# A second order of issue for a two-layer attention and token-mixing kernel: every operation's place and engine replaced by another list

## The chip, the core and the metric

The kernel runs on one core of a Trainium2 chip. A core has five engines with a queue of instructions each: TensorE (PE in the profile; its weight loads are shown as PEld), VectorE (DVE), ScalarE (ACT), GpSimd (POOL) and SyncE (SP), which here issues all DMA transfers. Engines wait for one another through semaphores. Matmul results go to PSUM, which has eight banks of 128 x 512 f32; everything else is in SBUF or in HBM.

The metric is the time of one execution on the device in microseconds; the median of several runs is compared. A profile is one further execution.

## The reference

Two kinds of block, each applied twice, with a residual: A is attention with a sliding window of 256 positions in 32 heads of 16 channels, B mixes over the 2048 positions (tokens), not over the channels.

```python
def _A_ref(x, wqkv, wo):
    B, S, D = x.shape                      # 1, 2048, 512
    H = 32; Dh = D // H; W = 256
    qkv = (x @ wqkv).reshape(B, S, 3, H, Dh).transpose(2, 0, 3, 1, 4)
    q, k, v = qkv[0], qkv[1], qkv[2]
    scores = jnp.einsum("bhqd,bhkd->bhqk", q, k) * (Dh ** -0.5)
    idx = jnp.arange(S)
    mask = (idx[:, None] - idx[None, :] >= 0) & (idx[:, None] - idx[None, :] < W)
    p = softmax(where(mask, scores, -1e9))
    o = jnp.einsum("bhqk,bhkd->bhqd", p, v)
    return o.transpose(0, 2, 1, 3).reshape(B, S, D) @ wo

def _B_ref(x, w1, b1, w2, b2):             # w1: 2048 x 1792, w2: 1792 x 2048
    h = layernorm(x)
    u = gelu(jnp.einsum("bsd,sf->bdf", h, w1) + b1)
    y = jnp.einsum("bdf,fs->bds", u, w2) + b2
    return y.transpose(0, 2, 1)

x = A_x
x = x + A(layernorm(x)); x = x + B(layernorm(x))
x = x + A(layernorm(x)); x = x + B(layernorm(x))
```

All inputs and the output are bfloat16.

## The kernel before

The activations x stay in SBUF (`x_sb`, 16 tiles of 128 positions). Each of the two layers is one A and one B.

*Attention.* The sixteen tiles are taken in four groups of 512. `qkv` (L530) transposes the normalised tiles (by DMA, or for the first group by PE with an eviction, L544, L551, L553), multiplies them with wqkv (`mm_group`, whose matmuls all stand under L508) and evicts q, k and v from PSUM. K is expanded to a block-diagonal form `kbd`, so that two heads share 32 rows: by POOL or DVE (`f_kz2`, L603) or by eight small DMA transfers on SP (`f_kz`, L598). V goes to `vb` by DMA (L628). `attention` (L656) then works in score groups: 8, 12 or 24 small matmuls into four banks (L682), two exponentials on ACT (L697), masks on POOL (L718), and, once several groups are there, the product with V (L735). The product's result is transposed, normalised and transposed again (L755 to L766, on DVE, with the multiplication on POOL or DVE). `wo_block` adds the output projection to x (L777) and begins the next normalisation.

*Token mixing.* `u_part` (L830) multiplies the normalised tiles that are there with pieces of w1, which SP loads into four buffers (`load_w1`, L791), and collects partial sums (L841, L843, L845). `u_last` (L849) does the rest, L856, and the gelu (L871). `y_block` (L889) multiplies with w2 (`load_w2`, L803) and adds to x (L897). y of layer 0 is made between the attention work of layer 1. So PE always has dense matmuls (all under L508 and L856) that can be put between the score groups.

*What sets the order.* The program first describes 2471 operations, each with its reads, writes and one to three ways of doing it (engine and function). Then a list that is written out in the file decides everything: `ORDER`, a compressed text, gives for each place in the order which of the operations left comes next and which of its ways is taken.

```python
for lo, hi in zip(raw[:n], raw[n:]):
    k, alt = divmod(lo + 256 * hi, 4)
    out.append((left.pop(k), alt))
```

`Graph.replay` (L175) goes through this list once. It appends each operation to the queue of its engine and gives it buffers and PSUM banks, as a rule those that have been free longest; whoever used a buffer last is added to what the operation waits for. `emit` (L196) writes the queues out with the semaphore waits that are needed (L242). So one list sets the order on five engines, the engine of each operation that has a choice, the order of the DMA transfers on SP's queue, and which bank each matmul group takes over from whom. The functions `mm_cost` to `pool_cost` (L253 to L265) play no part when the list is replayed.

Of the kernel before, what the change touches and what calls it, by code (L numbers as in the profile page):

```python
# [7 lines left out]
dt = mybir.dt  # L8
# [3 lines left out]
P = 128  # L12


ORDER = (
    'c-pmAJ&5br6~40X?7Q#nO}GI)P@x3{?t&H+(1HS5&;t=vsL+BI^uUD+2VA&tp@0`uxKQE31QjkE@Pdm8DB!|{3l}aNaN)v*3l}b?aN)v*3l}B~!Nmk}W'
    'Y2i)_hy&u%kCMCbfx=yzVn^$SnedODN2knQDjVp+hTzTLQLETf#aB><9Od%mi3M?<Bv@LI(W~R#HwZM-OBrR37wYfj;FKfJL}zKI<ekLOg9W^&=<wGB3'
    'R=#6~%)nwmRL-rY(OlolcVRY&xHdZ<Ch!jrmPC41BQ~iekCUzpNF4g3m0|v?rw^Hu#saOt_|LTvIvUP)eo!WHN!LEXxSPpQ@^amdmVOVhwR$y+16!*wJ'
    '}uJ`XnAcxyYhedpBcb)=ii^?EHy(u6P2LQxL<FyK2r9HeQ#M|Znj4FF*LcZyP3EEn?yg-M}4&bAs1M&r>~QP^NeBq?~`Znr6IJ8`eqlbO`$-gen$6Pnc'
    '|5%qY^8qHE>f38O5N_nxUR;$xc3aj-}R9?U)rA=|Sds7Vuwc1GKy;@kU(sEj<_`c_r$}q9+!6}16P|`F>EqIFW*wRLl?;!-{d~T-oH^gy9qmgK5ws!2l'  # L20
    'F*b(dDVnZDk*4XoLSa)?(*gi4g9nDuVzH;2w`4pXTXwf=iK1@6rMFrwLI6VuyGXk<j$@J}2qj4ZXwYh9u-R-_zdxnqw|Kp}%WSjV-fcI5?fbhutQ^Oyc'
    'zu7r_V)jBoVEA*-i_yz@hFb*axpOHi$UKs$78eG?GA<m*EM$zi_;!suIu)aq}go3UiG?EF2`}BRyUHwI2>BWzR@6XFs)vX%b8WHl_kcd5-yiVBUCCu_}'
    'w7z;i1W@YOFVFa8*-*xnPn61k{y*qI@Mu;{)9(NlV7fX1ha36i1HZ)M|b$3@a^Y`Z26li!v-dS!QqnyPcz{B104dGF)BFxDLh@rG-*LahggPuoJVqsn>'
    'G~R{(Ne84W8C2u_GhB+(Wn(-b9HlDMS!@I7lv<Tb+>bCn+s=x``xR93u5RxI1L3Iyn`X^<N`NJSVfGcoO_SsHaZ9kh86(EZw{gb1h}^(Xy4LVY#jLsLM'
    'VPNm)Mv}xu)WG_Z`Ba|dcb>>S5DJbjEXl5mv>I$b)wU-Tzuo5&-093_Oby6(3Zd*ery-jFrnz3m+u8SGwT=i5}byQ79Xyv$jWJ{`U@UbK@8TVvmIJE0b'
    'Y}LdCQ$#0<Sgn@IAy}bMu;LN~IErXZR1m=IsweZl&62lIdcARPG*UR6ir?P0l;1;CzkmykoC?^eQrS_|YPYmnO^g0e`#x^Okny$zYyjP;h7%YMevtvBP'
    'mz$pU{I|(z^a5yJis)H5~c52#YPwwi<L^D0K<ZyAZ6%K0%5Ui_=k)T33*KjB!!OAe!FjiDrovfTjP~s8mrX;lxs`@S<oEROK)#GwEdu%5aLFo0cs>!mL'
    'v@+>1&<N59kM#X!>8ZY(I?s@^{~9dW`W+?R!N5W!di5+v$|y#bPwsZnw5Qv?2fQR<QbfHlIu*ux<q5fqX?Sr2!p|+@WPNHk-{fL<P%&gDW6~-4>+?Qsp'
    '(``+GnJ7H=!cLYe0p4VJVL)@SwJc-(BVM%e3BR5eK62Wspa<tQy?0jkG!4<pw{UX}s~o2KV@t|N*L^C*BKdAjMCmY&Jy+A^(~X&7HQt^*Q!a6Namx{H_'
    'THvNb6cRu2rgGw2ex#D+sHC;C?$cn12iPS72I2kCErU4_g_ZoP;4Z~r!r~=vm$;0{lPxIMK*C(8}Rkbi24M!2E#Ar0cu<GDzV>U|*0gU5QKtYmao7e<*'  # L30
    'JMH%Uy}fVkK#%*t=>QJh?znDJPhfT&!>cNa6)`9W1tX|bE8c3g^SmXH#4$ipTnkb!C?tv6<PSbBaM!h6jQ<S}&x1nbh>)+EWm}lIvl()yQ&-yU2(i}4g'
    'hGWf4Fc7LsH<&Fqlk0g4}6@-kTtPnG=%c^aKJb87DLEZtJboGF_gjC4A#YHI2n&akj6n84u`{8x0^svT;xF23TqHRjEk75QKYIv-z%3rRw`p`V_%YLzU'
    '70EnPxq+EHzy<3<(kqN>#@G^B^k^4-bq|Xc)%Cw)gj0gjYyZJEa-$49eVm{LgWgi-TiE-a;)S{XXaEmrc}YpjMpt6+-H9^p~g}Mc646#)SevSSm7zNul'
    '8TmUYLllIfk6m1u4wdDao%3RS2g1`;BUkbof3#7t~3N)cfU=!*2N-Qs-F<Hpoz)qufS_a@$SJN4xfE!y)%8P$N_jgS(I;zkonQ|Le|Mgg1va>_??P$&j'
    'L2})5w0ZG^Mku6(_>xsB1mzr`z)%7-VbhRu=CO05g6{U}L9ceIG)D$RjzVF*M=TzD4#0R#S6AEcb(Po2}u(>)|t-!l+s^G!4w@l@O+>ujxBTvZPT?c*)'
    '+;(7C8cLBiE)582rKm<h40gbYHB_|0pf1a48b^B%icGZ`6w77ecZ;K9r5F}V6&(4#*hD}xw+8-O85M)THZ@Qc%>b$8Sv5OC_km?_y?S+Oze1mAf*^d-t'
    'n7BY;C6!^TUa<5Liy}d{=EL<*VDZG({;2{6XQJC@#Cv}{(7?<{AJhKKKrO~)x4aV%e{E?oAZ%B_9?pwr#JX<iBG2|xtwt96!68Ar#AQvo#&pXg@rd)8='
    'Tzw(7PW2_uLYWkEbx50e;-)3Ej+7Fai7(KJ*Om%blK&Yvu&uV_aS^e8CanrStuNBzhrQDEDLN<WBt`4F75Pa_EV3&+wi7xjM6Oo+h9RfS*U5L4929X`v'
    'qr;WZJ?Uj_7w0QGb2H!psrKRZ5;EPElhZfMqVlgoYnLTqwZxa3Y8MOWg0o&xi^@cHBStC0N!`5>X*;QUcWP6CoYzT_`Q<R9N(LsR(aAmm?kJCDwe=RT5'
    '{GZN&9sOVzs#eiJyH2dbli;L4_PUBP3VSL4#&xGUegqKKl9E(r6ik}_MU(!%Gf6c$_<po;#mmoO1{js1vX)}K8IzF!bzJx^hSxEpy$X$}*?2m9Ql2=mr'  # L40
    'p$va&J-lG0@Vwx&JY37fvnoFqypw*P&viNRvFl1nejyqCU;P&@A}f3<UcbgcKMe1)YX34@{o0QH7qHM$z5'
)

def begin_order(n):
# [932 lines left out]
```

## Time and profile before

| | |
|---|---|
| median of 3 runs | 440.39 us (440.28 to 440.48) |
| the profiled execution, own time | 441.33 us |
| its span, first to last instruction | 439.6 us |
| mean granted TensorE clock | 0.999 |
| score groups on PE / exponentials on ACT | 152 / 304 |
| median of one exponential of 128 x 1024 | 1.03 us |
| DMA traffic, mean | 103 GB/s |

In the profile, L508 means line 508 of the kernel. A line of a timeline gives start, duration, engine, line, what is written and read, and the number of instructions merged; in brackets the idle time before and what ended it. "issue" is idle time for which the profile shows no wait. Durations of matmuls overlap: the score matmuls use a quarter of the rows each and run four at a time. The stages are 0 to 22 us (start), 22 to 157 (attention of layer 0, with the projections and part of u between), 157 to 201 (the rest of B), 201 to 354 (attention of layer 1, with y of layer 0 and u of layer 1 between) and from 354 on B of layer 1 and the stores.

### The profile page before, as it was taken

The numbers are of one execution on the slowest core, as the hardware profiler recorded it, in microseconds if no ns is written. First come the engines' busy times: TensorE is split into PE (matmuls) and PEld (weight loads), VectorE is DVE, ScalarE is ACT, GpSimd is POOL, SyncE is SP. The second block draws the span as 40 slices with busy tenths as digits, with TensorE's granted clock in tenths as the row PEclk, the third lists the DMA queues.
The fourth block names the chain that finished last, engine by engine and source line by source line (L and its number), as shares of the span: only waits on it lengthen the run. The fifth ranks groups of instructions, "written<-read, shape, count | busy, mean of one in ns | idle before, by whom it ended". The sixth has DMA issues, their size and how long they took to land.

```text
span 439.6 us, 13924 instructions
## 1 busy us (share of the span) xinstructions
PE 423.1 (96%) x5992; PEld 187.3 (43%) x5992; DVE 306.8 (70%) x562; ACT 317.8 (72%) x364; POOL 234.2 (53%) x352
## 2 busy tenths in 40 slices
PE   8889888999999999999999999999999999999996
PEld 6444333344333444443444444443343444444443
DVE  6999898788894688665666797679977647522224
ACT  5999999999899921628799899999999960530000
POOL 4799779878876521011576577879876541000000
PEclk9999999999999999999999999999999999999999
DMA  8843233301233448323651333140312256854343
GB/s 241 242 87 60 55 90 62 70 14 46 73 98 84 127 135 237 86 82 92 135 123 39 82 61 85 28 99 15 80 41 70 73 156 170 233 172 132 90 128 119
DMA packets 101037, 45.22 MB, mean 103 GB/s; under 512 B 31216, under 2 KB 100976, under 8 KB 100976
## 3 DMA queue, kind: packets, MB, share of 16 engines
q1 hardware_dynamic: 100976, 44.34, 39.7%
q8 instruction: 47, 0.77, 0.8%
q14 instruction: 14, 0.11, 0.1%
HBM read 33.56 MB, written 2.10 MB: 81 GB/s over the span
## 4 chain that ended last, share of the span: by engine, by line
PE 77%; ACT 18%; DVE 4%; issue 1%; POOL 0%
PE PS L508 53%; ACT pt L697 18%; PE PS L856 8%; PE PS L682 8%; PE PS L735 6%; PE PS L391 1%; DVE kbd L577 1%; DVE stats L466 1%; DVE xh_sb L486 0%; DVE rl L755 0%; DVE vst L623 0%; PE PS L544 0%; ACT xhT L553 0%; DVE x_sb L897 0%; DVE agg L468 0%
## 5 line engine op out<-in xcount | busy, mean ns | idle before, releaser
L697 ACT ACTIVATE pt<-PS 128x1024 bf16<-128x1024 f32 (+1 forms) x304 | 281.7, 1040 | 15.1 <-PE PS L682 13.0
L718 POOL TENSOR_TENSOR pt<-pt,ldm 128x256 int32<-128x256 int32 (+2 forms) x270 | 177.2, 682 | 66.5 <-ACT pt L697 63.5
L508 PE MATMUL PS<-xh_sb,w1b 128*128 128x512 bf16 x280 | 69.5, 381 | 0.5 <-DVE xh_sb L486 0.3
L508 PE MATMUL PS<-xhT,wqkv 128*128 128x512 bf16 (+1 forms) x288 | 66.2, 357 | 2.5 <-ACT xhT L553 0.7
L508 PE MATMUL PS<-uT,w2b 128*128 128x512 bf16 (+1 forms) x294 | 68.2, 369 | 0.0
L682 PE MATMUL PS<-qT,kbd 32*128 32x256 bf16 (+4 forms) x1488 | 60.8, 251 | 6.2 <-ACT pt L697 3.2
L479 POOL TENSOR_TENSOR rstd<-agg,mhalf 128x2 f32<-128x2 f32 (+1 forms) x33 | 22.8, 692 | 62.4 <-DVE agg L468 62.3
L755 DVE STREAM_TRANSPOSE rl<-PS 128x1024 f32<-128x1024 f32 x32 | 39.8, 1243 | 19.9 <-PE PS L735 19.7
L897 DVE SCALAR_TENSOR_TENSOR x_sb<-PS,b2col,x_sb 128x512 bf16<-128x512 f32 x31 | 22.8, 747 | 42.9 <-PE PS L508 42.4
L682 PEld LDWEIGHTS PS<-qT,kbd 32*128 32x128 bf16 x1488 | 21.9, 92 | 65.6 <-ACT pt L697 46.3
L871 ACT ACTIVATE uT<-rl,b1col 128x512 bf16<-128x512 f32 x28 | 18.6, 714 | 41.3 <-DVE rl L867 41.0
L735 PE MATMUL PS<-pt,vb 64*17 64x320 bf16 (+4 forms) x2976 | 43.1, 251 | 2.2 <-DVE uT L841 0.5
L466 DVE BATCH_NORM_STATS2 stats<-x_sb 128x6 f32<-128x512 bf16 x64 | 43.2, 682 | 1.7 <-DMA x_sb<-in_A_x_dram 0.9
L508 PE MATMUL PS<-uT,pt 128*128 128x512 bf16 x168 | 41.4, 379 | 0.0
L508 PEld LDWEIGHTS PS<-uT,w2b 128*128 128x128 bf16 x294 | 27.2, 98 | 31.1 <-issue 3.5
L856 PE MATMUL PS<-xh_sb,w1b 128*128 128x512 bf16 x168 | 38.3, 379 | 0.0
L735 PEld LDWEIGHTS PS<-pt,vb 64*17 64x17 bf16 x2976 | 30.7, 84 | 17.5 <-issue 5.7
L508 PEld LDWEIGHTS PS<-xh_sb,w1b 128*128 128x128 bf16 x280 | 23.5, 97 | 33.0 <-issue 6.6
L508 PEld LDWEIGHTS PS<-xhT,wqkv 128*128 128x128 bf16 x288 | 23.9, 97 | 30.5 <-issue 5.3
L508 PE MATMUL PS<-wqkv,xhT 128*128 128x512 bf16 x128 | 33.4, 381 | 0.3 <-DVE kbd L577 0.3
L508 PE MATMUL PS<-wo_sb,oT 128*128 128x512 bf16 x128 | 32.7, 381 | 0.0
L486 DVE TENSOR_SCALAR xh_sb<-x_sb,agg,rstd 128x512 bf16<-128x512 bf16 x64 | 28.9, 469 | 4.9 <-POOL rstd L479 4.7
(59 smaller groups left out, 317.9 us busy)
## 6 DMA issues: line engine op xcount, KB each, us to landing
w1b<-in_B_w_dram SPq DMA_DIRECT2D x112, 128.0 KB, 2.9
w2b<-in_B_w_dram SPq DMA_DIRECT2D x70, 128.0 KB, 2.5
pt<-in_B_w_dram SPq DMA_DIRECT2D x42, 128.0 KB, 3.2
vb<-vst SPq DMA_DIRECT2D x64, 68.0 KB, 2.1
out_dram<-x_sb SPq DMA_DIRECT2D x15, 128.0 KB, 1.8
x_sb<-in_A_x_dram SPq DMA_DIRECT2D x3, 512.0 KB, 7.8
wqkv<-in_A_wqkv_dram SPq DMA_DIRECT2D x4, 256.0 KB, 4.8
kbd<-stg SPq DMA_DIRECT2D x64, 16.0 KB, 2.0
```

The source lines that it names most:

```text
L466: op("vector:stat", lambda e: e.bn_stats(st[:, 0:6], x_sb[:, t, :]), reads=[f"x{t}"], writes=[("st", i)], cost=dve_cost(512))
L479: op("gpsimd:rstd", lambda e: e.tensor_tensor(rstd[:, t0:t1, 0], agg[:, t0:t1, 1], mhalf[:, 0:1].to_broadcast([P, t1 - t0]), op=ALU.pow), ...
L486: op("vector:xh", lambda e: e.tensor_scalar(xh_sb[:, t, :], x_sb[:, t, :], agg[:, t, 0:1], rstd[:, t, :], op0=ALU.subtract, op1=ALU.mult), ...
L508: return e.matmul(o, lhsT=w, rhs=x, start=start, stop=stop, skip_group_check=True)
L682: last = e.matmul(bank(tt[r // 2], r % 2)[:, base + c0 * 64:base + (c0 + n) * 64], lhsT=kbd[32 * r:32 * r + 32, tk.slot, o, jj].rearrange( ...
L697: op("scalar:exp", lambda e, ts=ts, tp=tp, i=i, cols=cols: e.activation(probs(tp)[:, i, 0:cols, :], pair(ts)[:, :, 0:cols].rearrange("p r ...
L718: return e.tensor_tensor(v, v, m, op=ALU.mult)
L735: last = e.matmul(bank(t, h)[32 * r:32 * r + 17, i + q0 * 64:i + (q0 + n) * 64], lhsT=vb[64 * h:64 * h + 64, tk.slot, jj, 4 * o + r, :], r ...
L755: op("vector:od", lambda e, t=tod, tr=tr: e.transpose(rl[:, tr.slot:tr.slot + 2].rearrange("p a b -> p (a b)"), pair(t)), reads=[(tod, i) ...
L856: last = e.matmul(bank(tu, tt), lhsT=v()[:, sc - b0, k0 + tt * P:k0 + (tt + 1) * P], rhs=xh_sb[:, sc, :], start=(sc == b0), stop=(sc == NT ...
L871: op("scalar:gelu", lambda e, ft=ft, tt=tt: e.activation(uT[:, ft, :], rl[:, tmps[tt].slot], ACTF.Gelu_apprx_tanh, bias=b1col[:, ft:ft + 1 ...
L897: op("vector:resy", lambda e: e.scalar_tensor_tensor(x_sb[:, t, :], bank(ft), b2col[:, t:t + 1], x_sb[:, t, :], op0=ALU.add, op1=ALU.add), ...
```

## The change

The text of `ORDER` is replaced; nothing else differs. It has one line more, so all later lines of the new file have a number that is one higher.

```diff
 ORDER = (
-    'c-pmAJ&5br6~40X?7Q#nO}GI)P@x3{?t&H+(1HS5&;t=vsL+BI^uUD+2VA&tp@0`uxKQE31QjkE@Pdm8DB!|{3l}aNaN)v*3l}b?aN)v*3l}B~!Nmk}W'
...
+    'c-qBRJ&5Dl6~40X?A}f8d)y6LP(Tl~phAUSP(TTKpa*)OfC37rP~pM>J#gVd0TC2%z=a7aT&Qs2LWKh^T)0r-z!XlH!i5VLE~aqd!T}RpOfiLvDJC#Qj'
...
 )
```

Read back, both texts describe the same 2471 operations with the same dependencies. What differs:

| operations | engine before | engine after |
|---|---|---|
| K expansions (24) | POOL 10, SP 8, DVE 6 | POOL 7, SP 10, DVE 7 |
| normalisation after the product with V (32) | POOL 17, DVE 15 | POOL 18, DVE 14 |
| evictions of q, of k (first group, others), of v | ACT 8, 3, 3, 3 | ACT 8, 2, 2, 5 |
| evictions of the PE transposes (8) | ACT 4, DVE 4 | ACT 3, DVE 5 |

43 operations change their engine. The 152 score groups keep their sequence; the other PE operations move by a few places between them. A piece of PE's queue near 60 us of the profile before, by operation:

```
before: scores, 2 q, v | scores, v, 2 k | scores, V-product, V-product | scores, 2 wo | scores
after:  scores, v, 2 q | scores, v, 2 q | scores, 2 k, V-product | scores, V-product | scores, 2 wo
```

(q, k, v, wo: pairs of 512-column matmuls of these projections.) The weight loads on SP's queue and the vector work on DVE are reordered throughout.

More of the change, by code (lines that the diff above doesn't have):

```diff
@@ L15 @@
 ORDER = (
-    'c-pmAJ&5br6~40X?7Q#nO}GI)P@x3{?t&H+(1HS5&;t=vsL+BI^uUD+2VA&tp@0`uxKQE31QjkE@Pdm8DB!|{3l}aNaN)v*3l}b?aN)v*3l}B~!Nmk}W'
-    'Y2i)_hy&u%kCMCbfx=yzVn^$SnedODN2knQDjVp+hTzTLQLETf#aB><9Od%mi3M?<Bv@LI(W~R#HwZM-OBrR37wYfj;FKfJL}zKI<ekLOg9W^&=<wGB3'
-    'R=#6~%)nwmRL-rY(OlolcVRY&xHdZ<Ch!jrmPC41BQ~iekCUzpNF4g3m0|v?rw^Hu#saOt_|LTvIvUP)eo!WHN!LEXxSPpQ@^amdmVOVhwR$y+16!*wJ'
-    '}uJ`XnAcxyYhedpBcb)=ii^?EHy(u6P2LQxL<FyK2r9HeQ#M|Znj4FF*LcZyP3EEn?yg-M}4&bAs1M&r>~QP^NeBq?~`Znr6IJ8`eqlbO`$-gen$6Pnc'
@@ L20 @@
[L20 to L39, printed above, removed]
@@ L40 @@
-    '{GZN&9sOVzs#eiJyH2dbli;L4_PUBP3VSL4#&xGUegqKKl9E(r6ik}_MU(!%Gf6c$_<po;#mmoO1{js1vX)}K8IzF!bzJx^hSxEpy$X$}*?2m9Ql2=mr'
-    'p$va&J-lG0@Vwx&JY37fvnoFqypw*P&viNRvFl1nejyqCU;P&@A}f3<UcbgcKMe1)YX34@{o0QH7qHM$z5'
+    'c-qBRJ&5Dl6~40X?A}f8d)y6LP(Tl~phAUSP(TTKpa*)OfC37rP~pM>J#gVd0TC2%z=a7aT&Qs2LWKh^T)0r-z!XlH!i5VLE~aqd!T}RpOfiLvDJC#Qj'
+    '%<&|p4olbO$a%Re(sO%J?Hz*`L0J4#129TW2|CAFhaj>V~m((`Mz)4HnZK|SQayx@eN~4{hEoQ`7K{(`Y)C%EGyP`b9#M!ZR@tG8DC#rUFo_m<{jKqRm'
+    'R>jmdiPn`FA|uy<4*7V6n&=%T-tS>3p$B+1pfa>j~@i2kfo%K8mFG^&|-l!!!)TaU{o-r1zSxs;Z{Tu=(vw;HBB@P9!{IlEfa6`0#*ONLeR@cBium9;8'
@@ new lines @@
+    '+n+Kn)3Z13*ws_$<bado*^Y&I}mTCUdXHP1&;M5p>}CJ4f4q9~)$dR+kk1O~2ew>-~pc(>6i%xTT9p*>Njzf(q6lSEON4DHU_EbH}quIHennDr-76y>Z'
+    '39;O}s%XGC`1z`}7AZ#Y>Dj134D3m0)N3+?i7Dby%vr@gfO2$D@3uu(*I1F9a4Wl3k{C9j9)W8DQg(j|I@YC=slsdMsq0}%m*PG1%Y1i{TO@kIy4SI=X'
+    'O(j{DQ7TE242FGK!M+dt*&?n60?&J1zuzB^$Hs+$HC-cw6!X$lCUP4LcgRoD^Z`F?@9*xReG`S@B_`k<p?JAkZnw*2p6Aicc3WGTn~G^dq=4vp(QG!Io'
+    '9o4TZJMStnPsn56Qj{+%x3dz!<Y^Rux-}M@;?lQ!yMvd-CmzTf_1yyRI91&C^Ex#(r+d`Q#F9?SP)t*x!Qo`n~lalf*@`H67{;egd`0DNfL&`A+~MD0S'
+    'X)!@ZpV)DoOKe0C_r<@YMtu5j6=ZO4jd-A|0eC?WBy5w&OTCZpF>mgWR?&cC}imh;>n9tfDbb@H~&HRa8+GNv22?3E@>u)z)j>&;fEvF7>faVEbW7bzH'
@@ new lines @@
+    '}X5L^#0N=ZT>D+ys#Rsh#4UJwP}vH)~pE>@=;FGxJN1P^c)j3}z2MTFho-$UAnND#!q1E42L-gWV<1Qk%9Ob{;!-sBCJ=ZG@KLw!;pW_5dul4RXZRH#;'
+    'jrW~3~fcdP~>jBJ^A_VLYDILHd^B}El9r7ft>N=yQ2AxfUiZ3mSIyefE+jKn?Ik@hlk(=|9VYUe3RZ}wzrBbO@#)_&c4uvW-EX7n{^?)M7T(2#~S}ZgT'
+    'k|Ga7S(d~>R}#f;kxcD;fbALz_6Efq3W8Y!_80?SD7n9Pl*PhaRDZjk)79$lN?}9Ig1h>4mffsG0hC4&CV~))X84s*3EHWgB#C8Jfp8&i)S_4lz8AhKU'
+    '}bZt1vD67)N|co*X@AKp@t?<WJwZ6VY^XS?3fnM*D4j>C&U2^ij@SQLN*Lt6eS>B(`-;V+nSIBUGnb`cMEC+iMXnOMl4N}8j4H`8w>_LS&_5s5={+58j'
+    'qVz-L%Zsur;cT{?h6@e|DT}Jxv>pKO*J#L}ePJA5m2@Rnk-l!%)2gA$ucyzuC~)tiD<idKruY(8WbB0Wx=+4CnJP$Y`Nd<EydNhT_rR&FAy1M~GP<rYZ'
@@ new lines @@
+    '{QGK5A%x*S1uw3B=nX(L^v01RtJNy18W5DwzFp69fa1%O5vwxPe3v>LTI1~!|mCK`_s=enlgIJKJc9n^;7fwE8vrvPlf-Fm*e&<h|$#|>b(CI|s9X;P&'
+    '+9{=@knyR{2a8vX8ZPj*Q*fc;Hnl0Nl<GA0)Jr+5T-$7tiVf(3RAxM3SBq}4hUeD`wI7F_yUEx<ybHXnL;W8hMf})Bcw*=h+<MUAtsiV#2Gkw^zi!n$x'
+    'V*=>++U-t?w%h&yw^~`R1#VlDq@6Sq)ij$8*f)+rKx@>6J9X=!?F2Re4Q|#!vAzkgSphjST@U1(5IFWc%W-AU7T1E><Zo_n1k4+%;d(%dJM|_LkGX0=0'
+    '5}GUsxytph7lToHi6PrygI0@=kjo1O%Y@0@{%%id#erxKjRr3m<73S$Q454>1Z?@PUB%d%&)Fuux^&;X$nkdJ=`TkC+$?zTD)Juu%hj{ezmIje#P%$FT'
+    '-62TlUXQ9g@^+Hrvev4scD6Sfo-aig5Pu4yE_>{vL7z|MUJ{vAwZkZEl=gF-^||EQ>$j-2wPb^II3vI_~m4mSuVm4ic88sM8hNl!q#gBSm2KsL;(ywF+'
@@ new lines @@
+    'm~*7De9Yj0e~<awA3fhq_|QeT3~!uW#HFF2u-0wz3vu~{KdCW<_Sip+E}DPc^xo(l*OB8iY@Q(@xs2wjh84Pm2)K+&>l+zX;KifdtrP%ZFkH7`bP<RUm'
+    '>6@q*p1y#>Sy64{viJ<GI0m7#0z*WUm>z=D=gBnq#uA&d!fvQV!Y{<4|<AS7K9T5p_4cWcbWYu?hOeIiD${^txmF`dl)NL`5LHI#0TzllAwRpc8ZI`1F'
+    '5%5sRA7CaGgu!Ljy}Qf#Nr&fGc^iSiM|^S8cEiz#1+_GdYBl~~Pyz067zkAd$aY=BHsHrq==(JTQO(u>BV8_psmLz0`&|OUfllnP@fv-qz5dA5SFaJrJ'
+    'vO+L{vTSb_=0=c!rbF)8SP$o5AJd0VvH*nt@7bseht_Dz4-N6{y<da6Ng@*QVDY$cjo`OyNBnSXAVQV1Rs}6=PScn7sczv#p&dIYrhY-_xdr~ecvw1b2'
+    'spdmycTchldYaJQBh^I&#34`yf3fFph)kysLN|uG1Zg)%K$wb>gK<=-}5W?;QFMto&&>pqGxn94|;MeF#48NZrB7(veT@<rc>zJ<d5?hp<cMA8{P_Q~`'
@@ L42 @@
+    '$u;+~`S1AzXI?aR;p;)~M;Js$#qX{q$8w1fLOGo{k8b}n|kC(}NhVn05Sj6KZ9{60(cM>e^0;CBzqfm-bTVJ&K#`w@4n_d-wbvl@i1H~Yu2<7F*A>Cj7'
+    '+EkE54A(ajQluD&z&+~dLows%!yK206CUfVxwQE8M+#w3g?L*x?_A-l~zB+!3AEVyIQQiY_fb1EHhfrW*`M}$G;N|j5VJkl){u#B$7Jdx;Nq(N9e<moO'
+    'S{sk4aURC0`g~ycbLHtH4n7I-UKUOz1s!&M+WH_nM*-oulXO1xa3_9o96G6h!!q1wIL>|g2={NX=02C0|H4Wi-Tfq8A9dg;+T7!TcpNzu;`6ose<J)ZT'
+    'KY$r'
 )
```

## The prediction

> **What bounds the kernel now.** I read the page first, for which engine is full and when.
>
> ```profile
> PE 423.1 (96%) x5992; PEld 187.3 (43%) x5992; DVE 306.8 (70%) x562; ACT 317.8 (72%) x364; POOL 234.2 (53%) x352
> ...
> PE   8889888999999999999999999999999999999996
> ...
> ACT  5999999999899921628799899999999960530000
> ...
> PE 77%; ACT 18%; DVE 4%; issue 1%; POOL 0%
> ```
>
> TensorE (PE) is busy 423.1 of 439.6 us, so 16.5 us is all that an order could ever win, and the PE row shows it as eights in the first eight slices (88 us). In those same slices ScalarE (ACT) reads nine. The table of stages (PE busy is its second pair of columns, ACT its fifth) says the same in numbers.
>
> ```profile
> 22.00:91.00 69.00, 63.11 (x1350) 26.40 (x1351) 59.95 (x107) 67.08 (x73) 57.86 (x83) 1.00 0.36 68
> ...
> 201.00:301.00 100.00, 100.00 (x1613) 42.05 (x1617) 73.66 (x132) 92.55 (x105) 68.12 (x102) 1.00 0.38 83
> 301.00:354.00 53.00, 52.07 (x921) 21.29 (x909) 41.98 (x74) 51.38 (x57) 39.74 (x60) 1.00 0.25 62
> ```
>
> From 22 to 91 us the exponentials on ACT set the pace (67.08 of 69) and PE waits 5.9 us; from 201 to 301 PE has no idle time at all. So in layer 0 a gap on ACT is what costs, and in layer 1 up to 300 us only a PE wait does. The ACT timeline of layer 0 lists its gaps (in brackets, with what ended them).
>
> ```profile
> 22.43 29.88 ACT L697 ACTIVATE pt<-PS 128x1024 bf16<-128x1024 f32 x32 [0.49 <-PE PS L682]
> 52.91 9.27 ACT L697 ACTIVATE pt<-PS 128x1024 bf16<-128x1024 f32 x10 [0.60 <-PE PS L682]
> 62.92 37.30 ACT L697 ACTIVATE pt<-PS 128x1024 bf16<-128x1024 f32 x40 [0.74 <-PE PS L682]
> 100.39 9.27 ACT L697 ACTIVATE pt<-PS 128x1024 bf16<-128x1024 f32 x10 [0.17 <-PE PS L682]
> 110.05 9.39 ACT L697 ACTIVATE pt<-PS 128x1024 bf16<-128x1024 f32 x10 [0.39 <-PE PS L682]
> 120.48 25.95 ACT L697 ACTIVATE pt<-PS 128x1024 bf16<-128x1024 f32 x28 [1.03 <-PE PS L682]
> 147.35 7.44 ACT L697 ACTIVATE pt<-PS 128x1024 bf16<-128x1024 f32 x8 [0.93 <-PE PS L682]
> ```
>
> The sum is 4.35 us. PE's timeline around the two gaps at 62.92 and 120.48 shows what was late:
>
> ```profile
> 59.49 0.40 PE L682 MATMUL PS<-qT,kbd 32*128 32x192 bf16 x8
> 60.33 1.41 PE L735 MATMUL PS<-pt,vb 64*17 64x64 bf16 x96 [0.44 <-DVE stg L588]
> 61.67 0.36 PE L682 MATMUL PS<-qT,kbd 32*128 32x128 bf16 x5
> 62.53 0.34 PE L682 MATMUL PS<-qT,kbd 32*128 32x320 bf16 x7 [0.50 <-issue]
> ...
> 116.17 0.87 PE L735 MATMUL PS<-pt,vb 64*17 64x64 bf16 x56 [0.55 <-DVE uT L841]
> 116.97 0.40 PE L682 MATMUL PS<-qT,kbd 32*128 32x192 bf16 x8
> ...
> 119.32 0.23 PE L682 MATMUL PS<-qT,kbd 32*128 32x128 bf16 x3
> 120.05 0.39 PE L682 MATMUL PS<-qT,kbd 32*128 32x128 bf16 x9 [0.49 <-issue]
> ```
>
> Each time a product with V (L735) waits for VectorE (DVE) to empty the PSUM bank that it takes over (0.44, 0.55), and then a score group (L682) is cut in two by a wait that no semaphore explains (0.50, 0.49). The two cuts lie 2049 PE instructions apart (weight loads, matmuls and bare waits counted in program order), which is 8 x 256 + 1; the instruction queue moved 0.77 MB in 47 packets, so some 16 kB or 256 instructions each. I read them as PE running out of fetched instructions at the edge of a block.
>
> **The change, part by part.**
>
> *PE's own work.* Both orders hold the same 922 PE operations, and the 152 score groups in the same sequence. I price each operation by its usual start-to-next-start in the trace before: two 512-column matmuls 0.43 us, 0.53 when scores or V-products follow; a score group 0.33; a V-product of 40 or 56 matmuls 0.465 or 0.69, some 0.11 more when a dense matmul follows. Over all operations this gives 419.1 us for both (+0.06 for the new one: it has four more changes between kinds of matmul, 337 for 333). Work ahead of each score group differs by under 0.8 us in layer 0, so ACT is fed on the same schedule. Term: 0.
>
> *The start.* One eviction of xhT goes from ACT to DVE. Before, the two ran one after the other on ACT and ended at 6.88; on DVE the second takes 0.42 instead of 0.58, so the first projection can begin 0.17 earlier. Against it DVE now does one more statistics operation (0.65) ahead of the K expansion that the score group at 19.55 waits for. Walking the four queues by their rows I get that group about 0.1 late and the one at 21.98 on time, since it waits for a DVE queue that holds the same work. Term: 0, between -0.3 and +0.4.
>
> *The gap at 62.92.* The new order puts two dense matmul pairs ahead of the first V-product and the score group between the two V-products, so that the block's edge falls into the second product. From the start of the previous score group: two pairs 0.96, product 0.7, DVE's eviction (0.69) that the score group waits for 0.15, that is about 2.1 us plus 0.40 for the group itself, where before its last matmul ended 3.38 after. The previous exponentials end 2.69 after that start, so ACT sees no gap. If the edge costs its 0.50 again, it does so after the group, hidden behind 1.8 us of exponentials. Gain 0.7, between 0 and 0.74. The score group of the gap at 52.91 moves 0.2 nearer to its predecessor: gain 0.15, between 0 and 0.6. ACT is gapless from there to 91 us, so both reach the end.
>
> [...]
>
> *The gap at 120.48.* The V-product at 116.17 no longer takes the bank that was just filled: the 0.55 goes. But the block's edge stays in the same score group (after its fourth matmul, before after its third), and the fetch begins 2.45 us before PE resumes at 120.05. If the fetch isn't earlier, PE only reaches the edge sooner and waits longer. Gain between 0 and 1.03; I take 0.2, near the lower end, because the row at 120.05 names the later of the two waits.
>
> *Tight evictions.* A dense group that takes over a bank emptied only 0.76 to 0.86 us of PE work earlier lost 0.02 to 0.14 in the trace before, mean 0.09. Past 77 us there are six such pairs before and ten after: four more, +0.35. Lower bound 0 (ACT may wait anyway); upper bound 0.5 each, which is what the group at 21.98 lost when DVE began 0.57 late, so up to +5 for ten.
>
> *Engines changed.* 43 operations change engine. In layer 0 POOL loses four K expansions and gains two (1.36 each) and has one normalisation less (1.06); DVE is lighter by about 1 us between 20 and 62, where it is 92% busy; ACT trades one eviction each way. No idle time on the path is named for POOL except 0.4 us, so this is worth 0; cover is the other engines' slack.
>
> *SyncE's queue.* K expansions by DMA (L592, 5.9 us of issue each) go from five to seven in layer 0. One now stands ahead of four w1 loads near 135 us. From the matmul that frees the first of the buffers, the readers come 12.6 and 13.0 us of PE work later; the chain is 0.4 + 5.9 + two to four issues of 0.47 + a landing of 2 to 4.3 us (the slowest w1 rows near there), 9.3 to 12.5. It fits with 0.5 us to spare at worst. What is queued behind are w1 loads for the dense groups at 147 us; if one is late, PE waits for the rest of its landing. Term 0, up to +1. All other loads keep at least 4.3 us from release to reader, as before. The table load, the last matmuls and the last stores (the final half row 1.7 us after its issue) are as before.
>
> Sum: 0 + 0 - 0.7 - 0.15 - 0.2 + 0.35 + 0 = -0.7 us on the profiled 441.33 (span 439.6, 1.7 around it), so 440.6. That execution was 0.94 above the median of 440.39; on the median it makes **439.7 us**.
>
> **Rivals.**
>
> *Nothing arrives.* The gains are refilled by the next wait (the fetch at 120, a bank at 64): 440.4. For it: PE's slots are nearly full from 78 us on, and what comes early there waits again. Against: the gap at 62.92 lies in a stretch where ACT alone sets the pace.
>
> *All named waits go.* 0.74 + 0.60 + 1.03 = 2.4 us: 438.0. For it: both gaps begin with the same pair of waits, and the first of each pair is gone. Against: the second edge hasn't moved.
>
> *Late evictions (slower).* DVE empties banks in the order of its queue. If it begins them 0.5 late at half of the ten tight pairs, that is 5 x 0.5 = +2.5, less 0.7: 442.2. It decides once DVE starts more than about 0.3 us after its bank is full. For it: at 21.98 that happened, and DVE's order is new throughout. Against: beyond 91 us DVE is 74 to 80% busy and mostly waits for PE.
>
> *A late w1 load at 147 us (slower).* If two loads land 1 us past their spare time each: +2 - 0.7, 441.7.
>
> **How the numbers follow.** The forecast gets 0.45, with a range of its own of 439.0 to 440.3; nothing arrives 0.12; all waits go 0.20; late evictions 0.18; late loads 0.05. About 0.2% (0.9 us) is what a measurement of this kernel tells from no change, so the line is at 439.5: the forecast's range gives 0.17 to faster and 0.28 to same. Faster 0.17 + 0.20 = 0.37; same 0.28 + 0.12 = 0.40; slower 0.18 + 0.05 = 0.23. The range 437.9 to 442.0 leaves out the upper part of the late evictions and the best of the lower bounds.
>
> **What would show it.** The gap near 62.9 on ACT gone, the cut falling inside a V-product: right. A cut of 0.5 to 1 us in the score group near 120 still there with no wait before the V-product: the second step right. DVE-named waits of 0.3 and more on dense groups past 91 us: late evictions. PE waits on a w1 load near 147 us: the queue. It is wrong altogether if PE idle time before 140 us changes by more than 2 us.

## The result and the profile after

The changed kernel is slower: 444.04 us (442.80 to 444.57, six runs) against 440.33 us (440.13 to 440.91, six runs) for the kernel before on the same chip, ratio 1.0079 with a 95% interval of 1.0065 to 1.0093. The prediction was 439.7 us, range 437.9 to 442.0. The profiled execution took 444.2 us, span 442.4, mean granted clock 0.992 (before 0.999). One correction to the description of the change: 42 operations change their engine, not 43.

All line numbers of the changed kernel are one higher than before; the experiments below that have a helper of seven lines are seven higher again (`a_flat` has no helper). The page of the changed kernel, with the rows that were shown of before and the one of the granted clock:

```profile
PE 424.6 (96%) x5992; PEld 187.4 (42%) x5992; DVE 306.7 (69%) x565; ACT 316.9 (72%) x362; POOL 231.0 (52%) x347
...
PE   7779988999999999999999999999999999999996
...
ACT  4959999999999931616989999999999960440000
...
PEclk9969999999999999999999999999999999999999
...
PE 76%; ACT 14%; DVE 6%; DMA 1%; SPq 1%; issue 0%; POOL 0%
```

The third slice (22 to 33 us) stands out in three rows at once: PE 7, ACT 5 (before: 8 and 9), granted clock 6. The rest looks much like before. The ACT timeline of layer 0 shows the hole:

```profile
19.88 2.04 ACT L698 ACTIVATE pt<-PS 128x1024 bf16<-128x1024 f32 x2
26.13 1.94 ACT L698 ACTIVATE pt<-PS 128x1024 bf16<-128x1024 f32 x2 [4.21 <-PE PS L683]
28.49 1.94 ACT L698 ACTIVATE pt<-PS 128x1024 bf16<-128x1024 f32 x2 [0.42 <-PE PS L683]
30.58 16.74 ACT L698 ACTIVATE pt<-PS 128x1024 bf16<-128x1024 f32 x18 [0.15 <-PE PS L683]
47.57 46.31 ACT L698 ACTIVATE pt<-PS 128x1024 bf16<-128x1024 f32 x50 [0.25 <-PE PS L683]
94.19 18.62 ACT L698 ACTIVATE pt<-PS 128x1024 bf16<-128x1024 f32 x20 [0.31 <-PE PS L683]
113.20 9.39 ACT L698 ACTIVATE pt<-PS 128x1024 bf16<-128x1024 f32 x10 [0.40 <-PE PS L683]
122.85 26.18 ACT L698 ACTIVATE pt<-PS 128x1024 bf16<-128x1024 f32 x28 [0.25 <-PE PS L683]
149.85 7.44 ACT L698 ACTIVATE pt<-PS 128x1024 bf16<-128x1024 f32 x8 [0.83 <-PE PS L683]
```

The gaps that the prediction wanted gone are gone or small: 46.31 us without a break across the places of the old 0.60 and 0.74, and 0.25 where 1.03 stood. In their place is one gap of 4.21 us that ends at 26.13 us. PE's timeline there, and the granted clock in steps of 2 us (it is the number after the five engines' pairs; then come the DMA share and GB/s):

```profile
24.27 1.25 PE L736 MATMUL PS<-pt,vb 64*17 64x64 bf16 x64 [3.96 <-DMA vb<-vst]
25.46 0.61 PE L683 MATMUL PS<-qT,kbd 32*128 32x192 bf16 x12
```

```profile
22.00:24.00 2.00, 0.00 (x0) 0.00 (x0) 0.00 (x0) 0.00 (x0) 1.40 (x2) 0.58 0.52 107
24.00:26.00 2.00, 1.73 (x76) 1.14 (x76) 0.40 (x1) 0.00 (x0) 0.00 (x0) 0.50 0.57 138
26.00:28.00 2.00, 2.00 (x24) 1.20 (x24) 1.55 (x4) 1.87 (x2) 0.00 (x0) 0.50 0.46 64
28.00:30.00 2.00, 2.00 (x30) 0.80 (x21) 1.60 (x4) 1.58 (x3) 1.86 (x4) 0.72 0.51 103
```

The first V-product waits 3.96 us for the copy of V from `vst` to `vb` (L629, issued by SP); then PE works at half clock until about 29 us, a score group taking 0.61 where it takes 0.40 at full clock. Why the copy is late stands on SP's queue. Its timeline, before:

```profile
9.17 1.18 SPq L419 DMA_DIRECT2D wo_sb<-in_A_wo_dram  x1
10.39 2.36 SPq L791 DMA_DIRECT2D w1b<-in_B_w_dram  x3
15.12 2.67 SPq L628 DMA_DIRECT2D vb<-vst  x4
...
24.97 0.59 SPq L398 DMA_DIRECT2D bst<-in_B_b_dram  x1
```

and after:

```profile
8.96 1.16 SPq L420 DMA_DIRECT2D wo_sb<-in_A_wo_dram  x1
10.16 1.36 SPq L399 DMA_DIRECT2D bst<-in_B_b_dram  x1
11.56 8.33 SPq L792 DMA_DIRECT2D w1b<-in_B_w_dram  x4
20.01 2.68 SPq L629 DMA_DIRECT2D vb<-vst  x4
```

Two things came ahead of the copy: the load of the column b2 (`bst`, 2048 elements of 2 bytes, each to another place) and more w1 loads (six ahead of the copy instead of four). The issue of the w1 load right behind the column load alone lasts from 11.56 to 17.97, 6.4 us; none of the three in the kernel before took more than 1.4. The copy leaves 4.9 us later, and 3.96 us of that reach PE.

Where the time went, as the start of the same score group minus its start in the kernel before. The comparison uses a second profile of before (440.61 us, the run `before_again` below), which is nearer to its median than the first one (441.33). The new order also moves dense matmuls past score groups; the second column says how many pairs of them (0.43 us each) its list has put ahead of the group in excess of the list of before. Only rows with the same number there can be compared with each other.

| group starts at (before) | dense pairs more ahead | first profile of before | changed | last repaired order (`g_best`) |
|---|---|---|---|---|
| 15.8 | 0 | +0.06 | +0.14 | +0.42 |
| 25.3 | 1 | +0.02 | +4.80 | -0.20 |
| 27.6 | 0 | +0.01 | +4.37 | -0.60 |
| 49.7 | 1 | +0.03 | +4.60 | -0.20 |
| 52.5 | 0 | +0.01 | +3.97 | -0.84 |
| 68.7 | 0 | +0.80 | +3.94 | -0.66 |
| 114.4 | 0 | +0.78 | +3.93 | -0.27 |
| 120.8 | 0 | +0.78 | +3.15 | -1.05 |
| 146.1 | 0 | +0.77 | +3.28 | -0.94 |
| 199.6 | 2 | +0.76 | +4.11 | -0.10 |
| 213.3 | 0 | +0.76 | +3.32 | -0.90 |
| 250.9 | 0 | +0.82 | +3.46 | -0.76 |
| 349.1 | 0 | +0.73 | +3.43 | -0.63 |
| end of the span | | +0.72 | +3.57 | +0.02 |

So the change loses 4.4 us before 28 us and wins some 0.4 at 52 and 0.8 at 121. The first profile of before shows something else: between 62 and 69 us it lost 0.8 us that the second one didn't lose.

### The profile page after: what moved, and what is told of

It reads as the page before. It is cut to its first block, busy times and chain, and to the rows that moved or that the text cites. A ratio compares the mean times of both kernels' runs of the same rounds, so it can differ in the third digit from the quotient of the medians.

```text
span 442.4 us, 13933 instructions
## 1 busy us (share of the span) xinstructions
PE 424.6 (96%) x5992; PEld 187.4 (42%) x5992; DVE 306.7 (69%) x565; ACT 316.9 (72%) x362; POOL 231.0 (52%) x347
## 2 busy tenths in 40 slices
DMA packets 103341, 45.49 MB, mean 103 GB/s; under 512 B 33520, under 2 KB 103280, under 8 KB 103280
## 4 chain that ended last, share of the span: by engine, by line
PE 76%; ACT 14%; DVE 6%; DMA 1%; SPq 1%; issue 0%; POOL 0%
PE PS L509 52%; ACT pt L698 14%; PE PS L857 8%; PE PS L683 8%; PE PS L736 7%; DVE stats L467 1%; PE PS L392 1%; DVE xh_sb L487 1%; DVE kbd L578 1%; DMA w1b<-in_B_w_dram 1%; DVE x_sb L778 1%; DMA vb<-vst 0%; DVE uT L842 0%; DVE stg L589 0%; PE PS L545 0%
## 5 line engine op out<-in xcount | busy, mean ns | idle before, releaser
L698 ACT ACTIVATE pt<-PS 128x1024 bf16<-128x1024 f32 (+1 forms) x304 | 281.6, 1036 | 16.7 <-PE PS L683 15.8
L509 PE MATMUL PS<-uT,w2b 128*128 128x512 bf16 (+1 forms) x294 | 69.5, 370 | 0.0
L509 PE MATMUL PS<-xhT,wqkv 128*128 128x512 bf16 (+1 forms) x288 | 67.2, 361 | 1.4 <-DVE xhT L552 0.5
L509 PE MATMUL PS<-uT,pt 128*128 128x512 bf16 x168 | 40.5, 379 | 0.0
L509 PE MATMUL PS<-wqkv,xhT 128*128 128x512 bf16 x128 | 34.6, 384 | 0.3 <-ACT pt L698 0.3
```

What stands on the lines that cost most here:

```text
L509: return e.matmul(o, lhsT=w, rhs=x, start=start, stop=stop, skip_group_check=True)
L698: op("scalar:exp", lambda e, ts=ts, tp=tp, i=i, cols=cols: e.activation(probs(tp)[:, i, 0:cols, :], pair(ts)[:, :, 0:cols].rearrange("p r ...
```

## The experiments

Two theories on the start. The column-load theory: 2048 separate elements in the queue hold up whatever SP issues next until older traffic is through. The traffic theory: the additional w1 loads (128 KB each) fill the DMA engines, and the copy of V comes behind them. Most kernels differ from one of the two orders only by a few operations moved in the list, with one helper. Each median is compared with runs of the kernel before on the same chip, so medians of different experiments differ by some tenths for the chip alone (440.33 to 441.04 us for the kernel before). In the list of operations 19 and 18 are the loads of b2 and b1, 21 and 20 their conversions on DVE, 516, 518, 501 and 534 the four w1 loads, 62 and 96 the first and second copy of V, 163 the last of four transposes that SP issues between them.

```python
def move(order, ops, behind, anchor):
    at = dict(order)
    rest = [x for x in order if x[0] not in ops]
    k = [x[0] for x in rest].index(anchor) + (1 if behind else 0)
    return rest[:k] + [(i, at[i]) for i in ops] + rest[k:]
```

**Column load late (`a_b2_late`).**

```diff
 order = begin_order(len(g.ops))          # the changed order
+order = move(order, [19], True, 163)
```

> Changed order with only the load of the b2 column (2048 elements of 2 bytes) moved from ahead of the copy of the first V group to behind it and the four xhT transposes, its old place; the four w1 loads stay ahead of the copy. Column-load theory: the 6.4 us issue behind it goes, V arrives as before, the 4.0 us wait of the first V-product is gone, median 439.5 (438.9 to 440.0). Traffic theory (the six w1 loads fill the queue): the wait stays over 3 us, 443 to 444.

Measured: 440.67 us (439.95 to 444.60, twelve runs), ratio to before 1.0002 (0.9983 to 1.0021). Four w1 issues take 2.77 us, the copy leaves at 14.88. The wait doesn't go to zero: PE waits 1.37 us, because the copy, issued until 17.57, lands only at 21.55, behind half a megabyte of w1 (the view puts this wait down to a normalisation on DVE, but the product begins 0.13 us after the landing). So the column load makes most of the loss, and the traffic has a share of about 1 us of waiting.

**The four w1 loads late (`a_w1_late`).**

```diff
+order = move(order, [516, 518, 501, 534], True, 163)
```

> Changed order with the b2 column load where the change put it, and the four w1 loads that stood between it and the copy of V moved behind that copy and the transposes. Column-load theory: the next issue is now the copy of V itself, which is held until about 18 us instead of starting at 15; V lands 2 to 3 us earlier than in the changed kernel, the wait shrinks from 4.0 to 1 to 2.5 us, 441 to 442.5. Traffic theory: the wait is gone, 439.5.

Measured: 443.98 us (443.12 to 445.61), ratio 1.0074 (1.0054 to 1.0093): the loss stays. As the column-load theory says, the instruction that is held now is the copy itself, for four issues that take 2.7 us otherwise:

```profile
14.94 5.02 SPq L636 DMA_DIRECT2D vb<-vst  x4
```

Its first issue alone ends at 17.92, within 0.05 us of where the held w1 issue ended in the changed kernel, though it began 3.4 us later. The first V-product waits 1.16 us. The time itself doesn't decide between the theories, because most of it is a new wait: SP stays late, the second copy of V is issued at 30.39 instead of 26.15 and lands at 34.43, and PE waits for that one:

```profile
34.56 1.89 PE L743 MATMUL PS<-pt,vb 64*17 64x64 bf16 x128 [2.98 <-DMA vb<-vst]
```

A late w1 load costs this profile another 1.05 us at 154 us.

**Both late (`a_both_late`).**

```diff
+order = move(order, [516, 518, 501, 534, 19], True, 163)
```

> Changed order with the b2 column load and the four w1 loads all behind the copy of V and the transposes. Both theories: no wait at the first V-product, granted clock full from 22 to 30 us, and what is left is the sum of the other terms of the prediction, 439.5 (438.9 to 440.0) against 440.3 before. If neither cause holds, the wait stays and it is 444.

Measured: 444.50 us (440.92 to 445.89), ratio 1.0081 (1.0058 to 1.0104): a miss, and it taught the most. The first wait is gone, as both theories say. But the column load now stands right ahead of the second copy of V, whose four issues last 4.72 us (26.59 to 31.31); it lands at 32.80 and PE waits 2.25 us, in the best of the six runs. This profile doesn't show that the column load is what stretched these issues: in `f_xh` below they take 4.34 us with four w1 loads ahead and no column load. That it costs at this place is shown by the medians: `c_all`, which differs from this kernel by the place of the two columns and their conversions alone, takes 440.31 us. What the five slower runs (442.50 to 445.89) waited for is in no profile.

**Column load early in the order of before (`b_b2_early`).**

```diff
 order = begin_order(len(g.ops))          # the order of before
+order = move(order, [19], True, 15)      # 15: the load of wo
```

> Order of before with only the b2 column load moved to where the change put it, right behind the load of wo; three w1 loads then stand between it and the copy of V. Column-load theory: the w1 issue behind it is stretched to about 18 us, the copy of V starts near 19 to 19.5 instead of 15.1, the first V-product waits 3 to 4 us, median 443.5 to 444.5. Traffic theory: 4 KB more change nothing, 440.3.

Measured: 442.39 us (442.03 to 443.23), ratio 1.0035 (1.0023 to 1.0047). SP's timeline of this kernel:

```profile
9.54 1.37 SPq L405 DMA_DIRECT2D bst<-in_B_b_dram  x1
10.95 6.87 SPq L798 DMA_DIRECT2D w1b<-in_B_w_dram  x3
17.93 2.69 SPq L635 DMA_DIRECT2D vb<-vst  x4
```

4 KB moved by a few places stretch three w1 issues from 2.36 to 6.87 us, and the copy goes at 17.93 instead of 15.12. The size was over-estimated: with two w1 loads fewer ahead of it the copy leaves 2.1 us earlier than in the changed kernel, PE waits 1.33 and 0.49 us, the clock stays full (1.00 from 22 to 30 us), and the cost is 1.4 us and not 3.5.

**Same place, same bytes, fewer pieces (`a_flat`).**

```diff
-bst[:, NFT:], B_b2.rearrange("(t p) -> p t", p=P)
+bst[:, NFT:], B_b2.rearrange("(p t) -> p t", p=P)
```

> Changed order, the b2 load in its place between wo and the w1 loads, but read as 16 neighbouring values for each partition (128 pieces of 32 bytes) and not as 2048 elements of 2 bytes, so that b2 stands at other positions than the reference has it; same bytes, same order, all four w1 loads ahead of the copy of V. Column-load theory (the number of elements counts, not the place or the bytes): no 6.4 us issue, the copy of V starts near 15 us, the wait at the first V-product falls from 4.0 to 1.5 or less, 440 to 441. Rival (any extra load there, or the w1 loads behind it, holds the queue): 444 as in the changed kernel.

Measured: 440.33 us (439.35 to 442.89, twelve runs), ratio 0.9992 (0.9979 to 1.0005). SP's timeline, to be read beside that of the changed kernel:

```profile
10.45 1.41 SPq L399 DMA_DIRECT2D bst<-in_B_b_dram  x1
11.90 1.86 SPq L792 DMA_DIRECT2D w1b<-in_B_w_dram  x4
14.83 2.67 SPq L629 DMA_DIRECT2D vb<-vst  x4
```

With 128 pieces instead of 2048 the four issues take 1.86 us instead of 8.33, at the same place and with the same bytes. The number of pieces is the cause. A wait remains (2.33 us in the profiled run, 1.5 or less expected): the copy lands at 22.46, 5 us after its last issue, behind the w1 loads. The profiled run is the slowest of the twelve (442.89); what sets it apart is told under `f_xh`. The DMA traffic between 8 and 24 us (GB/s in steps of 0.4 us) shows what the pieces do; first the changed kernel:

```profile
GB/s 301 334 361 382 381 381 371 356 351 341 348 351 351 353 343 382 333 348 348 230 114 44 24 23 5 0 92 233 274 72 125 259 256 109 86 155 55 139 113 72
```

then `a_flat`:

```profile
GB/s 330 312 344 357 348 358 343 343 346 358 343 356 346 351 346 371 338 346 355 335 319 307 328 304 264 274 194 245 176 215 129 48 35 22 22 19 237 242 172 100
```

In the changed kernel the traffic runs at some 350 until 15.6, then falls to 24 and to nothing at 18: the single elements pass (1986 packets of under 512 bytes between 15.6 and 18 us, where `a_flat` has 197), and SP is still held while the engines run empty. In `a_flat` it goes on at 300 and more until 17.6.

**Both bias columns out of the way (`c_all`).**

```diff
+order = move(order, [516, 518, 501, 534], True, 163)
+order = move(order, [19, 18], True, 710)     # an idle stretch of SP, 101 us
+order = move(order, [20, 21], True, 717)
```

> Changed order, with the four w1 loads behind the first copy of V and the transposes, and the loads of both bias columns (b1, b2) put where SyncE's queue stands empty, about 101 us, their two conversions on VectorE near 130 us. Column-load theory: both copies of V arrive in time (no wait over 0.4 us at the first V-products), the other gains of the change reach the end, 439.0 to 440.0, and the spread of the runs shrinks. Rival (the new order itself, without the loads, is no faster): 440.5 to 441.5.

Measured: 440.31 us (439.78 to 442.80, twelve runs) against 440.71 (thirty runs), ratio 0.9995 (0.9982 to 1.0009). The first wait for V is gone in the profile (span 437.9; 438.9 in the second profile of before), and of the second little is left:

```profile
31.23 1.53 PE L743 MATMUL PS<-pt,vb 64*17 64x64 bf16 x128 [0.61 <-POOL rstd L487]
```

The view names POOL, but the second copy lands at 31.09 and the product begins 0.14 us later, as in the runs that waited for a copy. In `g_best` the same product waits for DVE's eviction of `stg`, which ends here at 30.96, so the copy costs some 0.2 us. The best five runs are 439.78 to 439.97, but three of twelve are 441.6 to 442.8. The repaired order is no slower than before; the expected 440.0 wasn't reached, and the spread didn't shrink.

**The columns out of the way in the order of before (`d_cols`).**

```diff
+order = move(order, [19, 18], True, 907)     # an idle stretch of SP, 107 us
+order = move(order, [20, 21], True, 952)
```

> Order of before, with only the loads of both bias columns (b1, b2) put where SyncE's queue stands empty, about 107 us, their two conversions on VectorE near 136 us. Column-load theory: in the order of before the b2 load stands at 25 us behind little traffic and costs only where it stretches the second copy of V (3.87 us of issue for 2.67), which has time to spare: no change, 440.3 to 441.0. If the loads cost in the order of before as well, it is 0.5 to 1.5 faster.

Measured: 440.71 us, the median of before, ratio 0.9996 (0.9987 to 1.0005). The loads as such cost nothing that could be measured; in the order of before the b2 column (24.97 us) stands behind little traffic (92 GB/s from 24 to 26 us). The second copy of V is right behind it, but its issues take 3.87 us in the first profile and 2.57 in the second, and in the second the product waits for POOL (0.36 us), 0.47 us after the copy has landed.

**The piece near 60 us by itself (`b_62`).**

```diff
 order = begin_order(len(g.ops))              # the order of before
+order = move(order, [445, 446], True, 357)   # two k products behind a score group
+order = move(order, [362], False, 348)       # a score group ahead of a V-product
```

> Order of before, with only this piece of TensorE's queue near 60 us as in the change: the two k products behind the next score group, and the score group near 62 us ahead of the second V-product of the pair. The prediction's step: the cut between two blocks of instructions falls into the second V-product, ScalarE's gap at 62.92 (0.74) is gone, and -0.7 reaches the end of layer 0. Rival (nothing arrives): the gap comes back in the next 60 us and the end moves by less than 0.2.

Measured: 442.09 us (441.87 to 442.55), ratio 1.0030 (1.0018 to 1.0041): slower, which neither side expected. PE's timeline there:

```profile
59.86 0.40 PE L689 MATMUL PS<-qT,kbd 32*128 32x192 bf16 x8 [0.81 <-ACT pt L704]
60.19 1.04 PE L515 MATMUL PS<-xhT,wqkv 128*128 128x512 bf16 x4
62.02 0.87 PE L742 MATMUL PS<-pt,vb 64*17 64x64 bf16 x56 [0.79 <-DVE stg L595]
```

Nothing dense is left ahead of the score group, so it waits 0.81 for ACT; the k products come later by that, DVE's eviction of the second follows, and the V-product waits 0.79 for DVE. In the changed kernel two q products stand ahead of that group and no such wait exists (its V-product runs at 64.75 with no idle time before it). The edit leaves these two q products out, so it doesn't isolate the piece; what the piece is worth by itself stays open.

**The kernel before, a second profile (`before_again`).**

> The kernel before, profiled a second time. Accident theory: the two cuts of 0.50 and 0.49 us in the score groups at 62 and 120 us, which the prediction took for a fixed property of the order, are smaller or gone, ScalarE's gap at 62.9 with them, and the execution takes 440.2 to 440.7 instead of 441.33. Rival (they are fixed by the order): both again within 0.1 us.

Measured: 440.61 us. ACT and PE timelines:

```profile
52.90 46.52 ACT L697 ACTIVATE pt<-PS 128x1024 bf16<-128x1024 f32 x50 [0.60 <-PE PS L682]
```

```profile
61.66 0.40 PE L682 MATMUL PS<-qT,kbd 32*128 32x128 bf16 x12
...
119.27 0.39 PE L682 MATMUL PS<-qT,kbd 32*128 32x128 bf16 x9 [0.49 <-issue]
```

The score group at 61.66 runs in one piece and ACT has no gap near 62.9. The cut at 120 is there again, with 0.49 us. Two more kernels have the same queue of PE: `d_cols` and `b_b2_early` have no cut near 62 either, and the one near 120 with 0.22 and 0.43. So the first was an accident of the first profile, the second belongs to the order, though its size varies. Each side was right about one cut. In all nine profiles of the changed order there is no cut at 120.

The DMA packets of the instruction queue (16384 bytes each; eight of them for the 2049 PE instructions between the two cuts, some 256 each) show the difference. At each of these cuts PE goes on 1.4 to 1.6 us after one of them ends. The packet of the first cut (the eighth of the run) begins at 60.17 in the first profile of before and at 56.93, 58.82 and 58.55 in the other three. The packet of the second (the sixteenth) ends at 118.51 and 117.80 in the two profiles of before, 1.5 us ahead of PE; in the changed kernel it ends at 118.56, 3.8 us ahead of the group at 122.39. What sets when such a packet begins isn't shown.

**The changed kernel again (`after_again`).**

> The changed kernel once more, beside the repaired one. Column-load theory: the 3 to 4 us wait for the copy of V and the stretched w1 issue are there in this execution too, 443 to 444.5. If they were an accident of the one execution that was profiled, the wait is gone here.

Measured: 444.27 us (443.35 to 449.33), ratio 1.0101 (1.0065 to 1.0138); the wait for the copy of V is 3.6 us in this profile, the w1 issue behind the column load 6.1. Not an accident.

**One normalisation moved (`f_xh`).** In two profiles (`a_b2_late`, `a_flat`) one operation on DVE took 4.35 us, in the five others of the changed order up to then 0.91. DVE's and POOL's timelines of `a_b2_late`:

```profile
246.09 4.35 DVE L494 TENSOR_SCALAR xh_sb<-x_sb,agg,rstd 128x512 bf16<-128x512 bf16 x1
```

```profile
245.80 1.05 POOL L769 TENSOR_TENSOR ul<-rl,rc 128x512 bf16<-128x512 f32 x1
246.81 3.48 POOL L726 TENSOR_TENSOR pt<-pt,ldm 128x256 int32<-128x256 int32 x5
```

It begins during a multiplication of POOL and ends 0.15 us after the last of five masks (250.29). Between the score groups at 250.9 and 276.6 us these two profiles lose 1.7 and 2.0 us, so the two profiled runs (442.67 and 442.89) stand near the top of their twelve for it.

```diff
 # the order of c_all
+order = move(order, [1594], True, 1381)      # the normalisation, to where POOL is idle
```

> The repaired order (w1 loads behind the first copy of V, bias columns at 101 us) with one normalisation on VectorE moved: the one near 245 us, which begins 0.3 us after a multiplication of POOL and took 0.91 us in four profiles and 4.35 us in two (to the end of five masks of POOL that follow without a gap), now stands two conversions later, where POOL is idle. If this race makes the spread of the repaired order: no run above 441, median 439.5 to 440.0, no normalisation over 1.2 us. Rival (the spread is DMA traffic): three of twelve runs over 441.5 as before, median 440.3.

Measured: 441.03 us (440.03 to 444.59, eleven runs), ratio 1.0001 (0.9984 to 1.0019). The operation took 0.40 us in the profiled run, but the spread stayed, in two groups (440.03 to 440.14; 441.03 to 441.49, one run at 444.59). As the only cause of the spread the race is refuted. The profiled run is of the second group, and PE's timeline shows what it lost:

```profile
32.67 1.52 PE L743 MATMUL PS<-pt,vb 64*17 64x64 bf16 x128 [1.63 <-DVE xh_sb L494]
```

The view names a normalisation, but that had ended long before; the second copy of V landed at 32.54 (in `c_all` at 31.09). Four w1 loads are issued right ahead of it.

**The w1 loads behind the second copy (`g_best`).**

```diff
-order = move(order, [516, 518, 501, 534], True, 163)
+order = move(order, [516, 518, 501, 534], True, 96)
```

> The last repaired order, with the four w1 loads moved once more, from ahead of the second copy of V (issued at 26.7 us) to behind it. If the runs of 441.0 to 441.5 come from this copy landing after 31.2 us because the w1 loads fill the DMA engines ahead of it (landing 31.09 and no wait in one profile, 32.54 and 1.6 us of waiting in another), they go: median 439.5 to 440.1, no run over 440.7, 0.6 to 1.0 below the kernel before. Rival (the copy's landing varies by itself): two groups of runs again, near 440.1 and 441.4.

Measured: 440.12 us (439.03 to 441.07, eleven runs) against 441.02 (440.61 to 441.48, fifteen runs), ratio 0.9979 (0.9970 to 0.9988). The second copy lands at 30.54 in the profiled run, ACT works without a break from 20.16 to 42.50, no run is at 441.1 or above, and the two groups are one. The top of the runs is 0.4 above what I expected. By its interval this kernel is faster than the one before, by 0.9 us. The profiled run (440.91) is the second slowest of the eleven, so the profile doesn't show where the 0.9 comes from.

## Why the prediction was wrong, step by step

- **SyncE's queue: the step that failed.** It was set to 0, up to +1 us, on the sentence "All other loads keep at least 4.3 us from release to reader, as before". That looked at loads and their readers only, priced each issue at its usual 0.47, and left out the copies of V, which go through the same queue. The column load's move ahead of the first copy was in the list and wasn't priced. It measured +4.4 us at 27.6 us. The first V-product starts 3.64 later (24.27 for 20.63 in the second profile of before, after 3.96 of waiting); the other 0.7 comes in while the granted clock is at 0.50. `a_b2_late` shows that this one load makes most of it, `a_flat` and `b_b2_early` show the mechanism, `g_best` that nothing else of that size is in the order.
- **The start: right in itself.** The walk through the four queues gave 0 (-0.3 to +0.4). The score groups up to 15.8 us begin between 0.7 early and 0.1 late in the changed kernel (the earliest has two dense pairs fewer ahead of it), and the one at 22 us is 0.36 and 0.65 early in the repaired orders `g_best` and `c_all`. The late one was SP, a fifth queue that the walk had not.
- **The gap at 62.92: no gain, and the mechanism isn't shown.** The signs came as predicted (no wait of the first V-product, the score group whole), but the score group is whole in the second profile of before too: the 0.74 was an accident of one execution. That the edge now falls into a V-product, where it would be hidden, no run tests. The sum also took the gap off twice: 441.33 stood 0.94 above the median largely because of it (0.8 us between 62 and 69 us), and the gain was subtracted first and the 0.94 afterwards.
- **The gap at 52.91: right, under-sized.** Taken 0.15 with an upper bound of 0.60; measured 0.4, from 4.37 to 3.97 between rows with the same work ahead. All nine profiles of the changed order gain 0.3 to 0.4 between the groups at 38.5 and 52.5 us.
- **The gap at 120.48: under-sized.** Taken 0.2; measured 0.8. I expected the cut in the score group to stay and to wait longer. It is gone: the group at 122.39 of the changed kernel is one piece of 12, while `before_again` still has 0.49. The prediction kept the fetch where it was ("If the fetch isn't earlier"); it ends as early as before on the clock, in a kernel that is 3.9 us later there, so it is earlier for PE.
- **Tight evictions: no sign of the +5.** PE's waits that name DVE are 0.4 us or less from 60 us on in the changed kernel. The 0.83 us that the table shows between 146 and 200 us are no loss: the new order has two dense pairs (0.87 us) more ahead of the group at 199.6, and at 213.3 the difference is back at 3.32.
- **Late w1 load at 147 us:** 0.2 us of waiting for w1 past 143 us in all. The term 0 was right for this profile; in `a_w1_late` a load was 1.05 us late at 154 us, so the upper bound of +1 was needed.
- **Smaller readings.** The PE row has a nine in its fourth slice and the ACT row a five in its first, and the work ahead of a score group in layer 0 differs by up to two dense pairs (0.87 us, at 47.8), not by under 0.8. None of these changes the sum.

With the copies of V in time, the order is worth 0.9 us (`g_best`, 0.5 to 1.3 by its interval), where the prediction said 0.7 below the median of before. That agreement is partly luck. The terms behind it are others, 0.4 and 0.8 instead of 0.15 and 0.2 and nothing at 62.92, and `g_best` moves the columns, four w1 loads and one normalisation besides. Nor does its profile keep the gain: it stands 0.63 ahead at 349 us and 0.02 behind at the end, 0.5 of which is waiting for two w1 loads (356 and 368 us). The profile of `c_all`, one of its five best runs, does end 0.9 ahead.

## What to carry to other kernels

Before an order is priced, list for every queue of DMA issues what stands ahead of each transfer that an engine waits for, and count pieces, not bytes: 4 KB in 2048 pieces held the queue for 6.4 us, the same 4 KB in 128 pieces for nothing that could be seen. When two orders are compared by the start of the same group, first count the work that each has put ahead of it. A stall found in one profile is a property of the order only if a second profile shows it again, and a correction from that profile to the median must not be subtracted beside the stall that makes it up. In a start with as much to load as here, a load that nobody reads for 50 us (b2 is read at 63.2 us in the changed kernel) belongs behind the first copies, not in front.

## What the runs showed of the hardware

- An element-wise load in a full queue held the issue of the next transfer until the traffic had almost ended: one issue lasted 6.41 us in the changed kernel (until 17.97, as the traffic went from 23 GB/s to 0), 5.92 in `b_b2_early` and 2.98 in `a_w1_late`, where it began later; behind little traffic (24.97 us, before) the next issue took 0.84. Long issues come without a column load too: one of the second copy took 2.38 us in `f_xh`, behind four w1 loads. The column went as one packet per piece: 103341 packets in the changed kernel and 101421 in `a_flat`, 1920 fewer, which is 2048 less 128. How these packets hold the next issue isn't shown.
- The clock: with PE idle for 3.96 us the granted clock went to 0.50 for some 6.8 us (the four windows above), the last 4.9 of them with PE at work. A wait of 2.98 us (`a_w1_late`, 0.87, 0.50 and 0.77 in the windows from 34 to 40 us) and one of 3.6 us (`after_again`, 0.85, 0.50 and 0.80 from 24 to 30) brought it there for some 3.4 us each; in both it fell only after PE was at work again. After 2.33 us (`a_flat`, mean clock 1.000) and 2.25 us (`a_both_late`, 1.00 in the windows from 22 to 60 us) it stayed full. What the granted clock goes by isn't shown.
- The normalisation on DVE near 245 us, which starts inside a POOL operation, ended some 0.15 us after that operation (0.91 us in all, five profiles; at 250.66 after 250.51 in the changed kernel) or some 0.15 us after a whole burst of POOL operations behind it (4.35 us, two profiles; at 250.44 after 250.29 in `a_b2_late`), with the same order of these operations. What holds it there isn't shown. Moved to where it didn't start inside such a stretch, it took 0.40 us in both profiles (`f_xh`, `g_best`).
- In the five profiles of the order of before and of `b_62`, PE stopped inside a score group for 0.22 to 0.50 us with no wait that the profile shows, six times in all, and each time it went on 1.4 to 1.6 us after the end of a 16 KB packet of the instruction queue (at 62.53 after 61.05 and at 120.05 after 118.51 in the first profile of before). That PE ran out of fetched instructions there is the prediction's reading; no run shows it.
